# States' factors on VectorE instead of in TensorE's turns, and eight matmuls of zeros for each attention unit

## The chip, the cores and the metric

One core of a Trainium2 chip runs the whole kernel as one program. The metric is device time in microseconds; lower is better. The number for the kernel before is the median of three runs.

## The reference

Three stages follow one another. The attention reads x (4 batches, 8 heads, 512 tokens, 64 wide) against 32 states a head, both ways. The two results are joined to 2176 rows of 512. A dense layer with a Mish activation follows, and then a layer of eight experts of which each row takes the one with the best score.

```
scores = scale * x @ state.T ; a  = softmax(scores)  ; xread = a @ state
scores2 = scale * state @ x.T; a2 = softmax(scores2) ; sread = a2 @ x
x = concat([xread, sread]) as (2176, 512)
x = mish(x @ w_in) @ w_out
out = gate * (relu(x @ w1[e]) @ w2[e]),  e = argmax(cosine(x, expert_emb) / tau)
```

Both softmaxes divide by their sum plus 1e-9. The change touches only a2, the states' softmax.

## The kernel before

The attention is cut into eight units, one for each batch and half of the heads. A unit passes four steps. `s1` turns x on TensorE (tiles `xt`, copied to `xT` by ScalarE) and multiplies it by the turned states into the scores `sc`, which ScalarE copies to `ss`. `s2` makes both softmaxes: for the tokens' one GpSimd subtracts the maximum `mx`, ScalarE takes the exponential, GpSimd multiplies by the reciprocal sums `sm`. For the states' one TensorE turns the scores into `sb` (line 339), VectorE takes the maximum `mb` (line 342), ScalarE makes `a2` and the sums (line 346), and VectorE makes reciprocals of these (line 353). In the kernel before VectorE then makes a diagonal matrix `dg` of the reciprocals (line 355). `s3` turns `a` into `at` (line 368), and multiplies `a2` by `dg` into `a2t` (line 366), which turns and scales in one go. ScalarE copies that to `a2T` (line 371). `s4` multiplies it by x into `sr` (line 385), and VectorE places the result.

The loop over t calls `s1` of unit t, `s2` of unit t-1, `s3` of t-2 and `s4` of t-3, and one `convert_w`. It takes a block of the 64-bit weights w_in or w_out, loaded into one of two buffers, and makes two float parts of it: one pass on ScalarE (line 97), one on GpSimd (line 100), two on VectorE (line 71), and a split on ScalarE and GpSimd. Eight of 32 blocks are converted within the attention, the others beside the first steps of the dense layer.

The tiles that TensorE writes lie in few buffers. `xt`, `sb`, `at` and `a2t` of all units share four, under the tag `acc`; later the dense layer's sums lie there. `sc` has one buffer, shared with the first products of the dense layer (tag `ms`). A tile keeps its buffer from its first writer to its last reader.

The order of the instructions on each engine isn't that of the code. A planner lays them out ahead, up to the last part of the expert layer, by the durations that it assumes: an instruction goes to its engine's queue when its inputs and its buffer are due, the earliest in the code first. The order of each queue is fixed in the program. `warm(n)` is n matmuls of a 128x128 tile of zeros `wz` (bf16); it is called twice ahead of the units, with 30 each.

Of the kernel before, what the change touches and what calls it, by code (L numbers as in the profile page):

```python
# [8 lines left out]
F32 = mybir.dt.float32  # L9
# [6 lines left out]
ALU = mybir.AluOpType  # L16
# [5 lines left out]
P = 128  # L22
# [30 lines left out]
def body(tc, x, state, w_in, w_out, ee, tau, w1, w2, out):  # L53
    nc = tc.nc
    T, V, A, G, Y = nc.tensor, nc.vector, nc.scalar, nc.gpsimd, nc.sync
    stack = ExitStack()

    def pool(name, bufs=1, **kw):
        return tc.tile_pool(name=name, bufs=bufs, **kw)

    def tsc(o, i, s1, op0, s2=None, op1=None):
        if op1 is None:
            V.tensor_scalar(out=o, in0=i, scalar1=s1, scalar2=None, op0=op0)  # L63
        else:
            V.tensor_scalar(out=o, in0=i, scalar1=s1, scalar2=s2, op0=op0, op1=op1)
# [7 lines left out]
    def split(hi, lo, src, eng=None):  # L73
        A.activation(hi, src, AF.Copy)  # L74
        (eng or V).tensor_tensor(out=lo, in0=src, in1=hi.bitcast(F32), op=ALU.subtract)  # L75
# [34 lines left out]
    with stack:  # L110
# [7 lines left out]
        wz = const.tile([P, P], BF16, name="wz")  # L118
# [8 lines left out]
        ident = const.tile([P, P], F32, name="ident")  # L127
# [110 lines left out]
        def f32r(n, i, name):  # L238

            return xpool.tile([P, 512], F32R, tag=f"x{n}{i}", name=name)  # L240
# [25 lines left out]
        def attention(meanwhile):  # L266
            pa = ExitStack()
            tmp = pa.enter_context(pool("pa"))
# [21 lines left out]
            for h in range(4):  # L290
                q, r = divmod(h, 2)
                hs = slice(h * NST, (h + 1) * NST)
                o = SBD[hs, :, q, r * D : (r + 1) * D]
# [34 lines left out]
            def s2(u):  # L328
                d = ns[u]
                ss = d["ss"]  # L330
                v = ss.rearrange("p (g n) -> p g n", n=NST)
                mx = tmp.tile([P, 16], F32, tag="mx", bufs=2, name=f"mx{u}")
                V.tensor_reduce(mx, v, axis=AX, op=ALU.max)
                a = tmp.tile([P, 512], F32, tag="a", bufs=2, name=f"a{u}")
                av = a.rearrange("p (g n) -> p g n", n=NST)
                G.tensor_tensor(out=av, in0=v, in1=mx.unsqueeze(2).to_broadcast([P, 16, NST]), op=ALU.subtract)
                o = ps.tile([P, 512], F32, tag="acc", bufs=4, name=f"sb{u}")
                for j in range(KT):
                    T.transpose(o[:, j * P : (j + 1) * P], ss[:, j * P : (j + 1) * P], ident)
                A.activation(a, a, AF.Exp, scale=SCALE)  # L340
                mb = tmp.tile([P, 1], F32, tag="mb", bufs=2, name=f"mb{u}")
                V.tensor_reduce(mb, o, axis=AX, op=ALU.max)
                tsc(mb, mb, -SCALE, ALU.mult)
                a2 = tmp.tile([P, 512], F32, tag="a2", bufs=2, name=f"a2{u}")
                sb = tmp.tile([P, 1], F32, tag="sb", bufs=2, name=f"sbs{u}")
                A.activation(a2, o, AF.Exp, scale=SCALE, bias=mb, accum_out=sb)
                sm = tmp.tile([P, 16], F32, tag="sm", bufs=2, name=f"sm{u}")
                V.tensor_reduce(sm, av, axis=AX, op=ALU.add)
                tsc(sm, sm, 1e-9, ALU.add)
                V.reciprocal(sm, sm)  # L350
                G.tensor_tensor(out=av, in0=av, in1=sm.unsqueeze(2).to_broadcast([P, 16, NST]), op=ALU.mult)
                tsc(sb, sb, 1e-9, ALU.add)
                V.reciprocal(sb, sb)
                dg = tmp.tile([P, P], F32, tag="dg", bufs=2, name=f"dg{u}")
                tsc(dg, ident, sb, ALU.mult)
                d.update(a=a, a2=a2, dg=dg)

            def s3(u):
                d = ns[u]
                for n, key in enumerate(("a", "a2")):  # L360
                    o = ps.tile([P, 512], F32, tag="acc", bufs=4, name=f"{key}t{u}")
                    for j in range(KT):
                        js = slice(j * P, (j + 1) * P)
                        if n:

                            T.matmul(o[:, js], d[key][:, js], d["dg"], start=True, stop=True)
                        else:
                            T.transpose(o[:, js], d[key][:, js], ident)
                    if n:
                        t = d["a2T"] = tmp.tile([P, 512], F32, tag="a2T", bufs=2, name=f"a2T{u}")  # L370
                        A.activation(t, o, AF.Copy)
                    else:
                        if u < 2:
                            xh[0, u], xl[0, u] = f32r("h", u, f"xh0{u}"), f32r("l", u, f"xl0{u}")
                            split(xh[0, u], xl[0, u], o)
                        A.activation(AT[u // 2][:, u % 2, :], o, AF.Copy)
# [21 lines left out]
            for t in range(NU + 3):  # L398
                if t == 4:
                    load(3)  # L400
                if t < NU:
                    s1(t)
                if 0 <= t - 1 < NU:
                    s2(t - 1)
                if 0 <= t - 2 < NU:
                    s3(t - 2)
                if 0 <= t - 3 < NU:
                    s4(t - 3)
                for _ in range(t > 0):
                    if len(order) > len(order0) - FIRST:  # L410
                        convert_w()
                if t == 4:
                    embeddings(tmp)
                meanwhile(t)
# [579 lines left out]
        for g, (c, f) in enumerate(steps):  # L994
# [18 lines left out]
            if at == 2 and r:  # L1013
                pc, pf, _ = RUNS[r - 1]
# [130 lines left out]
```

## Time and profile before

| what | value |
|---|---|
| median of three runs | 733.88 us |
| the three runs | 731.34, 733.88, 737.31 us |
| the profiled execution | 731.85 us |
| its span in the trace | 730.1 us |
| granted TensorE clock, mean | 0.98 of full |

The span is the time from the first to the last instruction in the profile; 1.75 us of the profiled execution lie outside of it. PE is TensorE's matmul, PEld its weight load, DVE VectorE, ACT ScalarE, POOL GpSimd, SP the engine that issues loads. Times of the rows are microseconds from the start of the span, unless ns is given.

### The profile page before, as it was taken

How to read it: one execution, taken by the hardware profiler on the slowest of the kernel's cores; microseconds unless marked ns; L12 is line 12 of the kernel's file. 1: busy time of each engine (PE TensorE's matmuls, PEld its weight loads, DVE VectorE, ACT ScalarE, POOL GpSimd, SP SyncE). 2: the span in 40 equal slices, each digit the busy share in tenths (PEclk: the TensorE clock that was granted, in tenths of full speed). 3: DMA queues.
4: the chain of work that ended last, by engine and by line, in shares of the span. 5: the costliest groups of instructions: out<-in, count | busy, mean ns of one | idle time of the engine just before them, and what ended most of it. 6: DMA issues, size and time to landing. Idle time of an engine off the chain costs nothing.

```text
span 730.1 us, 11305 instructions
## 1 busy us (share of the span) xinstructions
PE 696.7 (95%) x3681; PEld 582.7 (80%) x3681; DVE 466.9 (64%) x969; ACT 456.3 (63%) x794; POOL 193.7 (27%) x165
## 2 busy tenths in 40 slices
PE   8789999999999999999999979799999999999994
PEld 8789877778888888888887867677888888888883
DVE  5987898897575865656567994573444752257741
ACT  5877989988697777656776776612434541246640
POOL 2785356651000210300002264212111312123101
PEclk9998999999999999999999999799999999999998
DMA  7652143430010100001000167305415631266530
GB/s 196 155 156 88 59 145 115 145 116 0 1 58 0 59 1 1 0 1 59 15 0 1 58 191 220 111 30 173 146 58 178 248 135 58 73 204 244 192 133 17
DMA packets 45499, 70.12 MB, mean 96 GB/s; under 512 B 23402, under 2 KB 23402, under 8 KB 45428
## 3 DMA queue, kind: packets, MB, share of 16 engines
q1 hardware_dynamic: 42068, 59.29, 25.2%
q0 software_dynamic: 3360, 9.99, 4.1%
q8 instruction: 31, 0.51, 0.3%
q14 instruction: 40, 0.33, 0.1%
HBM read 60.33 MB, written 9.98 MB: 96 GB/s over the span
## 4 chain that ended last, share of the span: by engine, by line
PE 40%; issue 24%; DMA 13%; DVE 9%; ACT 8%; POOL 3%; SPq 2%; POOLq 0%; DVEq 0%; ACTq 0%
DMA out<-ys,ix 8%; PE acc L106 6%; PE acc L107 6%; PE acc L108 6%; PE h L106 3%; PE h L107 3%; PE h L108 3%; DMA w<-in_moe_w_in 2%; DMA w<-in_moe_w_out 2%; DMA es<-in_moe_w 2%; PE lg L562 1%; SPq L285 1%; PE m L106 1%; PE m L108 1%; PE m L107 1%
## 5 line engine op out<-in xcount | busy, mean ns | idle before, releaser
L106 PE MATMUL acc<-woh,gh 128*128 128x512 f32 x272 | 110.0, 408 | 6.2 <-ACT gh L74 6.2
L107 PE MATMUL acc<-wol,gh 128*128 128x512 f32 x272 | 109.2, 403 | 0.0
L108 PE MATMUL acc<-woh,gl 128*128 128x512 f32 x272 | 95.9, 400 | 0.2 <-DVE gl L75 0.2
L936 POOL DMA_INDIRECT out<-ys,ix x21 | 21.1, 1007 | 195.4 <-DVE ys L63 187.9
L106 PE MATMUL hp<-w1h,xth 128*128 128x512 f32 x168 | 68.9, 410 | 0.0
L106 PE MATMUL y<-w2h,hth 128*128 128x512 f32 x168 | 68.0, 405 | 0.8 <-ACTq L877 0.8
L106 PEld LDWEIGHTS acc<-woh,gh 128*128 128x128 f32 x272 | 52.0, 191 | 20.1 <-ACT gh L74 9.1
L476 ACT ACTIVATE er<-h,mb__103 128x512 f32<-128x512 f32 x68 | 46.7, 686 | 33.8 <-PE h L108 31.7
L108 PE MATMUL hp<-w1h,xtl 128*128 128x512 f32 x168 | 67.3, 401 | 0.0
L107 PE MATMUL hp<-w1l,xth 128*128 128x512 f32 x168 | 67.2, 400 | 0.0
L107 PE MATMUL y<-w2l,hth 128*128 128x512 f32 x168 | 66.5, 396 | 0.4 <-DVEq L877 0.4
L108 PE MATMUL y<-w2h,htl 128*128 128x512 f32 x168 | 66.7, 397 | 0.0
L74 ACT ACTIVATE hth<-ht 128x512 fp32r<-128x512 f32 x42 | 23.0, 596 | 65.2 <-PE ht L920 62.0
L108 PEld LDWEIGHTS acc<-woh,gl 128*128 128x128 f32 x272 | 51.2, 190 | 13.0 <-DVE gl L75 1.8
L107 PEld LDWEIGHTS acc<-wol,gh 128*128 128x128 f32 x272 | 52.3, 192 | 11.0
L74 ACT ACTIVATE xth<-gt 128x512 fp32r<-128x512 f32 x21 | 12.4, 594 | 73.2 <-PE gt L894 73.2
L482 DVE TENSOR_TENSOR er<-er 128x512 f32<-128x512 f32 x56 | 40.0, 715 | 27.4 <-ACT er L476 27.4
L505 ACT ACTIVATE h<-er,mb__103 128x512 f32<-128x512 f32 x68 | 47.2, 695 | 10.5 <-DVE er L482 7.8
L106 PE MATMUL h<-xh,mh 128*128 128x512 f32 x128 | 51.2, 400 | 0.2 <-ACT xh L74 0.2
L107 PE MATMUL h<-xl,mh 128*128 128x512 f32 x128 | 50.4, 393 | 0.4 <-DVE xl L75 0.4
L108 PE MATMUL h<-xh,ml 128*128 128x512 f32 x128 | 50.2, 392 | 0.0
L506 ACT ACTIVATE er<-er,mb__103 128x512 f32<-128x512 f32 x68 | 49.2, 725 | 1.3
(435 smaller groups left out, 1704.7 us busy)
## 6 DMA issues: line engine op xcount, KB each, us to landing
sg<-in_moe_w SPq DMA_DIRECT2D x48, 512.0 KB, 6.4
w<-in_moe_w_in SPq DMA_DIRECT2D x16, 512.0 KB, 4.0
w<-in_moe_w_out SPq DMA_DIRECT2D x16, 512.0 KB, 3.3
es<-in_moe_w SPq DMA_DIRECT2D x32, 256.0 KB, 3.6
xn<-in_x SPq DMA_DIRECT2D x32, 128.0 KB, 3.4
x1d<-x SPq DMA_DIRECT2D x13, 256.0 KB, 3.4
x1d<-part SPq DMA_DIRECT2D x4, 256.0 KB, 2.9
xg<-x1d,perm POOLq DMA_INDIRECT x21, 3.7
```

The source lines that it names most:

```text
L74: A.activation(hi, src, AF.Copy)
L106: T.matmul(o, lh, rh, start=first, stop=False)
L107: T.matmul(o, lh, rl, start=False, stop=False)
L108: T.matmul(o, ll, rh, start=False, stop=last)
L285: Y.dma_start(XN[b][:, g, :, r * D : (r + 1) * D], src[g, r])
L476: A.activation(z, h, AF.Tanh, scale=0.5, bias=mb_[:, 0:1])
L482: V.tensor_tensor(out=z, in0=z, in1=z, op=ALU.mult)
L505: A.activation(r, z, AF.Square, scale=QS, bias=mb_[:, 1:2])
L506: A.activation(z, z, AF.Square, scale=QS, bias=mb_[:, 2:3])
L562: T.matmul(o[:, j], xt[:, k * P : (k + 1) * P], enT[:, k, :].unsqueeze(1).to_broadcast([P, 8, NE]), start=k == 0, stop=k == KT - 1)
L936: G.indirect_dma_start(out=out[:, :], out_offset=bass.IndirectOffsetOnAxis(ap=ix, axis=0), in_=y, in_offset=None, bounds_check=NTOK - 1, o ...
```

## The change

VectorE no longer makes the diagonal matrix. It multiplies `a2` (128x512) in place by the reciprocal sums, and TensorE turns `a2` in the same way as `a`. Ahead of the four turns of the scores of each unit, eight matmuls of zeros are written into the first quarter of the same tile `sb`, which the first turn then overwrites.

```diff
                 o = ps.tile([P, 512], F32, tag="acc", bufs=4, name=f"sb{u}")
+
+                for _ in range(8):
+                    T.matmul(o[:, 0:P], wz, wz, start=True, stop=True)
                 for j in range(KT):
                     T.transpose(o[:, j * P : (j + 1) * P], ss[:, j * P : (j + 1) * P], ident)
...
                 V.reciprocal(sb, sb)
-                dg = tmp.tile([P, P], F32, tag="dg", bufs=2, name=f"dg{u}")
-                tsc(dg, ident, sb, ALU.mult)
-                d.update(a=a, a2=a2, dg=dg)
+                tsc(a2, a2, sb, ALU.mult)
+                d.update(a=a, a2=a2)
...
-                        if n:
-
-                            T.matmul(o[:, js], d[key][:, js], d["dg"], start=True, stop=True)
-                        else:
-                            T.transpose(o[:, js], d[key][:, js], ident)
+                        T.transpose(o[:, js], d[key][:, js], ident)
```

## Rows read from the trace of the kernel before

**Rows 1.** Busy us by stage (instructions): PE, PEld, DVE, ACT, POOL; then granted clock.

```profile
17.50:62.00 44.50, 38.66 (x311) 37.05 (x310) 39.28 (x93) 34.43 (x70) 33.99 (x29) 0.92 0.55 156
62.00:165.00 103.00, 97.82 (x506) 80.11 (x505) 88.26 (x136) 93.52 (x168) 53.62 (x48) 0.98 0.32 108
165.00:420.00 255.00, 255.00 (x1318) 214.49 (x1318) 173.33 (x407) 185.26 (x327) 31.20 (x14) 1.00 0.06 18
```

**Rows 2.** Chain that ended last, from 17 to 67 us: start, length, what.

```profile
25.55 0.20 DVE dg L63
...
28.28 0.51 DVE dg L63
...
52.45 1.20 DVE dg L63
53.65 1.47 DVE wc07x L71
...
57.84 1.63 DVE wc10x L71
...
59.58 3.27 DMA w<-in_moe_w_out
```

**Rows 3.** Timeline of unit 2's turns: start us, length us, engine, instruction.

```profile
34.69 0.61 PE L368 MATMUL at<-ident,a 128*128 128x128 f32 x4
35.13 1.06 PE L366 MATMUL a2t<-dg,a 128*128 128x128 f32 x8
```

**Rows 4.** Line 63, VectorE, 15 to 70 us: ns min/median/max.

```profile
L63 DVE TENSOR_SCALAR sm<-sm x8: 156/174/1126, 15.0 to 67.3; 128x16 f32<-128x16 f32 x8
L63 DVE TENSOR_SCALAR sbs<-sbs x8: 140/153/154, 15.5 to 65.0; 128x1 f32<-128x1 f32 x8
L63 DVE TENSOR_SCALAR dg<-ident,sbs x8: 236/287/1200, 16.6 to 65.4; 128x128 f32<-128x128 f32 x8
L63 DVE TENSOR_SCALAR en<-en,er x1: 694/694/694, 36.1 to 36.1; 8x512 f32<-8x512 f32 x1
```

**Rows 5.** Groups by line and shape, 0 to 76 us: instructions, busy us, mean ns, idle.

```profile
L294 DVE COPY SBD<-stc 32x512 f32<-32x512 f32 x2 | 0.8, 420 | 0.1
```

**Rows 6.** Groups of VectorE alone, 17.5 to 62 us.

```profile
L63 DVE TENSOR_SCALAR dg<-ident,sbs 128x128 f32<-128x128 f32 x6 | 2.9, 476 | 0.0
```

**Rows 7.** Timeline of the start: the matmuls of zeros and the first turns.

```profile
0.99 4.43 PE L124 MATMUL wp<-wz 128*128 128x128 bf16 x52 [0.99 <-DVE wz L119]
...
5.25 0.60 PE L303 MATMUL st<-ident,SBD 128*128 128x128 f32 x4
...
7.12 0.50 PE L124 MATMUL wp<-wz 128*128 128x128 bf16 x6
```

**Rows 8.** Who waited for whom, 10 to 76 us: total us, times, longest.

```profile
PE xt L317 <- ACT a L346: 2.3, 1, 2.3
...
PE sb L339 <- ACT ss L325: 1.9, 1, 1.9
...
PE sb L339 <- ACT a2T L371: 1.4, 1, 1.4
```

**Rows 9.** Busy us around the low clock, columns as in Rows 1.

```profile
51.00:52.00 1.00, 0.00 (x0) 0.00 (x0) 1.00 (x3) 0.70 (x2) 0.43 (x1) 1.00 0.36 66
...
54.00:55.00 1.00, 1.00 (x11) 1.00 (x11) 1.00 (x1) 1.00 (x2) 0.92 (x2) 1.00 0.00 0
55.00:56.00 1.00, 1.00 (x7) 1.00 (x7) 1.00 (x3) 0.13 (x1) 0.83 (x2) 0.53 0.00 0
...
61.00:62.00 1.00, 1.00 (x7) 1.00 (x7) 0.96 (x4) 0.60 (x1) 0.00 (x0) 0.56 1.03 410
62.00:63.00 1.00, 1.00 (x11) 1.00 (x10) 1.00 (x3) 0.00 (x0) 0.00 (x0) 1.00 0.15 49
```

**Rows 10.** TensorE alone, 5.25 to 9 us: length, busy us (instructions), clock.

```profile
5.25:9.00 3.75, 3.75 (x41) 1.00 0.88 198
```

## The prediction

> **What bounds the kernel now.** I read the busy time by stage first, then the chain that ended last within the stage that the change touches, then the prices of its instructions, then who waits for whom there, then the clock. The stages differ. From 165 to 420 us TensorE is busy without a break [rows 1]; nothing that the change touches lies there, so that stage can only be moved as a block. From 62 to 165 us TensorE is busy for 97.8 of 103 us, ScalarE for 93.5 and VectorE for 88.3: 5.2 us of slack on TensorE. The attention's steady part is 17.5 to 62 us. VectorE is the fullest engine there, 39.3 of 44.5 us; TensorE shows 38.7, GpSimd 34.0 [rows 1]. In this part the chain that ended last passes mostly over VectorE, with loads of weights and GpSimd between: the diagonal matrix itself is on it at 25.55, 28.28 and 52.45 us, and the passes over the weights behind it [rows 2]. TensorE's turns aren't on it. So the stage goes at the pace of VectorE's queue, and this is where the change adds work; what it takes away is TensorE's.
>
> **The change part by part.**
>
> *Turns.* A unit's multiplication by the diagonal takes eight instructions and 1.06 us, the plain turn beside it four and 0.61 us [rows 3]. The change gives back 0.45 us of TensorE a unit, 8 x 0.45 = 3.6 us. As TensorE isn't on the chain, I count 0 of it.
>
> *Zeros.* Eight more matmuls of 128x128 a unit, 64 in all. At the start 52 of the same kind took 4.43 us, 85 ns each; six in a row took 0.50 us. One takes some 0.22 us from start to end, an estimate from 0.50 - 5 x 0.056, so six that follow each other by 56 ns fit too [rows 7]. A unit pays 8 x 0.056 = 0.45 to 8 x 0.085 = 0.68 us, all units 3.6 to 5.4 us. That eats what the plain turns save: TensorE's sum is 0 to +1.8 us, and its 5.8 us of idle time in the stage [rows 1] covers it. Without that cover it costs 1.8 us.
>
> *VectorE.* The diagonal (128x128) goes: median 0.287 us, mean 0.476 in the stage [rows 4, 6]. A product of 128x512 by a column comes. The nearest row is the same line with the same kinds of operands in place, 512 long: 0.694 us [rows 4]. Its length would leave no doubt, but it has 8 rows and is a single one beside a busy GpSimd. From below, a plain copy of 512 from the same memory took 0.420 us, at a time without GpSimd [rows 5]. From above, a pass of 512 long took 1.63 us in this stage [rows 2]. I take 0.694, as operation and operands are the same and GpSimd is busy for three quarters of the stage. A unit pays 0.694 - 0.287 = 0.41 us; from 0.420 it would be 0.13, and from 1.63 against the mean of 0.476 it would be 1.15. Six of the eight units have this step in the stage [rows 6]: 6 x 0.41 = 2.4 us, bounds 0.8 and 6.9. Three of these six stand on the chain now [rows 2], so 1.2 us is the least that I expect on the path; VectorE's 5.2 us of idle time can hide the rest. I take 1.8, the middle. The two other units lie outside of the stage and I count them at nothing: VectorE waits in the first, and in the last the dense layer's first steps run beside it; without that cover they add 0.8 us.
>
> A rule of the Trainium skill speaks for a lower price: VectorE: DVE Perf Modes, section Mode 2×_2P, says that a tensor-by-scalar operation between SBUF tiles runs at two elements a cycle even in fp32, since it reads one tensor through both ports. The copy of 0.420 us agrees and the product of 0.694 us doesn't, one instance each; by the rule the stage's 2.4 us would be 0.8.
>
> *Order within the unit.* The turn of `a2` now waits for the product instead of for the diagonal: 0.41 us later, and 0.45 us shorter. `a2T` is as late as before, and the product waits for nothing that the diagonal didn't wait for, so nothing new is queued behind it. No transfer is moved in the code.
>
> *Where the zeros land.* They need only `wz` and a free buffer under `acc`. The planner draws such instructions forward: of the 60 zeros of the two warm-ups, 52 run ahead of the first state turn, though 30 stand behind it in the code [rows 7]. So the eight zeros can stand well ahead of the turns of the scores, and `sb` then holds its buffer from there on. Buffers are short already: at 22.39 us the turns `xt` of a later unit waited 2.3 us for ScalarE's exponential over `sb`, its last reader, and once the turns of the scores waited 1.4 us for the copy of `a2t` [rows 8]. Both are waits for a buffer, as neither reads the other's data. Where the zeros meet such a wait, their 0.45 to 0.68 us comes behind it, ahead of the turns. I count one such case that VectorE doesn't hide, +0.5 us.
>
> *Sum.* 1.8 + 0.5 + 0 = +2.3 us at the end of the attention. TensorE's 5.2 us of slack from 62 to 165 us could swallow it, but ScalarE and VectorE are full there too [rows 1]; I let it through. The profiled execution of 731.85 us becomes 734.2; on the median, which lies 2.03 us higher, 733.88 + 2.3 = 736.2, and I forecast 736. The three runs of before span 6 us, so some 1% (7.3 us) is what can be told from no change.
>
> **The rivals.**
>
> *A: the zeros hold the buffers (slower).* Four buffers serve five tiles a unit. If `sb` takes one early in every unit, the wait of 2.3 us that is in the trace once comes back in others. For it: that row, and the pull forward of rows 7. Against it: `xt`, of the unit ahead, comes first in the code. It decides from three units on, since VectorE's slack of 5.2 us [rows 1] hides two. In five units it costs 5 x 2.3 = 11.5 us against the present layout: 745.
>
> *B: the zeros keep the clock up.* TensorE's clock falls to half from about 55 to 61.5 us and the instructions in a step of 1 us from 11 to 7; ahead of it TensorE did nothing from 51 to 52 us, where it waited 1.9 us for `ss` [rows 8, 9]. Eight zeros fill 0.45 to 0.68 us of that wait. If that holds the clock at 2.4 GHz, the 6.5 us at 1.2 GHz become 3.3, and up to 3.3 us are won if TensorE then leads. Against it: VectorE and a load are on the chain there [rows 2]. 736.2 - 3.3 = 732.9; with the cheap product (0.8 x 0.75 = 0.6 for 1.8) 731.7. I call it 732.
>
> *C: the turns let the clock fall.* From 5.25 to 9 us TensorE ran turns, zeros and the scores' matmuls at a granted clock of 1.00 [rows 10], and the one fall followed an idle stretch [rows 9]; the trace gives no sign that turns alone are too little. If they were, three more units would have a stretch like that from 55 to 61.5 us: 3 x 3.3 = 9.9 us of TensorE, of which its 5.8 us of idle time in the stage hides about half: 736.2 + 5 = 741. The Trainium skill, TensorE: Matmul & The Clock Gate, section Part 4: PE-mode transpose, has such a rule: turns aren't counted as activity as matmuls are, and the change makes turns of 32 products. By that rule the time is C's; rows 10 don't decide it, as real matmuls are among them.
>
> *D: a luckier layout.* The planner lays the whole program out anew, to the end of the dense layer. If the two buffer waits (2.3 + 1.4 us) and the wait for `ss` (1.9 us) fall away [rows 8], 5.6 us are won: 736.2 - 5.6 = 730.6, or 728 with the clock's 3.3 us where half of these overlap. More would have to come from 62 to 165 us, where TensorE has 5.2 us to lose.
>
> *E: nothing on the path.* VectorE's slack hides all of it: 734.
>
> **How the numbers follow.** Forecast 0.42 (733 to 739), E 0.12 (734), A 0.18 (740 to 746), C 0.07 (741), B 0.11 (732), D 0.10 (725 to 731). The range leaves out the outer parts of A and D: 727 to 746. Faster by over 1% is below 726.5: only the better third of D and layouts that I can't see, 0.08. Slower by over 1% is above 741.2: most of A, half of C, 0.18. Within 1%: 0.74.
>
> **What would show it.** The a2 product at line 63: near 0.69 us alone, or 0.42. The turns into `a2t`: four instructions, 0.61 us. In the stage to 62 us VectorE's busy time up by some 2 us and the dense layer's first `h` matmuls later by as much. For A: more waits of `xt` or `at` for ScalarE's exponential over `sb`, with the zeros far ahead of the turns in TensorE's queue. For B and C: the granted clock from 50 to 62 us, and at other places. The prediction is wrong if the new layout moves the loads of weights, and with them the end of the stage at 165 us, by more than the whole sum; or if TensorE, not VectorE, sets the pace of the units.

## The result and the profile after

The changed kernel takes 739.14 us (median of 12 runs, 734.51 to 742.68), the kernel before 732.37 us (12 runs beside them, 730.97 to 737.31): ratio 1.010, interval 1.0083 to 1.0116. It is slower by 6.8 us, clear of the noise. The forecast was +2.3 us, which the prediction itself put below what can be told from no change. The profiled execution of after took 739.43 us, span 737.7 us; the one of before 731.85 us, span 730.1 us.

**What came as worked out.** TensorE's part has the sizes of the forecast. The rows are from the timeline of after, unit 3 (columns as in [rows 3]; in brackets the idle time ahead and what ended it):

```profile
31.02 0.61 PE L340 MATMUL sb<-wz 128*128 128x128 bf16 x8 [1.51 <-ACT a2T L369]
31.47 0.61 PE L342 MATMUL sb<-ident,ss 128*128 128x128 f32 x4
...
35.88 0.60 PE L366 MATMUL a2t<-ident,a 128*128 128x128 f32 x4
36.31 0.60 PE L317 MATMUL xt<-ident,xn 128*128 128x128 f32 x4
39.49 1.09 PE L317 MATMUL xt<-ident,xn 128*128 128x128 f32 x4 [2.57 <-ACT a L349]
```

The turns into `a2t` are four instructions of 0.60 us where there were eight of 1.06 [rows 3]; eight zeros take 0.45 us to the next instruction. The 1.51 us that stood ahead of the turns of the scores [rows 8, 1.4 us] now stands ahead of the zeros, so these come behind the wait, not into it. One wait of `xt` for the exponential over `sb` is there, as before: it ends at 39.49 us instead of 22.39, and is 2.57 us long instead of 2.3.

VectorE's part came as worked out too, in its sum. The rows name the product `a<-a,sbs`, as the digits of names are left out (`a2` reads `a`). The first fence groups VectorE in the stage from 17.5 to 62 us (columns as in [rows 6]); the second is the busy time by stage (columns as in [rows 1]):

```profile
L63 DVE TENSOR_SCALAR a<-a,sbs 128x512 f32<-128x512 f32 x6 | 5.2, 870 | 0.0
```

```profile
17.50:62.00 44.50, 36.42 (x330) 34.67 (x328) 40.74 (x86) 32.28 (x66) 33.75 (x29) 0.96 0.54 145
62.00:165.00 103.00, 95.01 (x488) 77.59 (x488) 86.63 (x137) 90.52 (x163) 49.58 (x47) 0.98 0.32 108
165.00:420.00 255.00, 254.73 (x1307) 214.26 (x1308) 174.01 (x402) 186.16 (x329) 32.76 (x16) 0.99 0.05 16
```

Six products take 5.2 us where six diagonals took 2.9 [rows 6]: +2.3 us, forecast +2.4. The chain that ended last (start, length, what) shows what of it lies on the path, and what else does:

```profile
26.70 1.16 DVE a L63
...
29.22 1.04 DVE a L63
...
33.76 4.26 DMA w<-in_moe_w_in
38.10 0.35 ACT wc04x L97
38.66 0.78 ACT a L349 x2
39.49 1.09 PE xt L317 x4
...
41.09 0.96 PE sb L340 x8
...
45.12 1.80 PE sc L323 x16
...
55.05 1.40 DVE a L63
...
59.23 3.14 DMA w<-in_moe_w_out
```

The products on the chain are 3.60 us, the diagonals were 1.91 [rows 2]: +1.7 us, forecast 1.8. Between them stands what the forecast had at 0.5 us: a load of weights that lands at 38.02 us, the conversion `wc04x` that waited for it on ScalarE, the exponential queued behind that, and the turns `xt` that wait for the exponential.

What the forecast had not: from 39.49 to 46.92 us the chain stays on TensorE, with the eight zeros of a unit on it for 0.96 us, and TensorE's granted clock is at half from 39.6 to 43.0 us. In a second trace of the same kernel (e8, below) the chain is on TensorE from 39.37 to 55.94 us, with the clock at half from 39.0 to 52.7. In the two traces of the kernel before TensorE has nothing, and 2.5 us, of the chain from 17 to 60 us.

**Where the time is.** I cut each trace at two instructions of TensorE: the start of the first matmul of the routing scores `lg`, and the start of the last product `m` on line 106. Behind that `m` come the last sums of the dense layer and the experts' part, to the end of the span. From `lg` to `m` it is 197.4 to 197.6 us in every kernel of this study: that block only moves. The rows of after for `lg` and `m` (each with its first and last start), and those of before:

```profile
L560 PE MATMUL lg<-enT,xt x8: 217/274/275, 220.8 to 225.7; 128*128 128x64 f32 x8
L106 PE MATMUL m<-wih,STh x128: 277/281/562, 64.4 to 418.3; 128*128 128x256 f32 x128
```

```profile
L562 PE MATMUL lg<-enT,xt x8: 217/274/276, 215.9 to 220.8; 128*128 128x64 f32 x8
L106 PE MATMUL m<-wih,STh x128: 277/281/448, 61.7 to 413.4; 128*128 128x256 f32 x128
```

So 4.9 us are lost by there, and 737.7 - 418.3 = 319.4 against 730.1 - 413.4 = 316.7 us from `m` on: 2.7 us more are lost in a part that the change doesn't touch. Two further profiled executions (e7 and e8, below), of before (217.5, 316.8) and of after (220.4, 319.4), give means: an early loss of 3.9 and a late one of 2.65 us, 6.6 of the 6.8 measured. The late values of a kernel agree within 0.2 us, the early ones of before differ by 1.6.

The two pairs of traces don't lose the early part in the same way. Up to `lg`, TensorE is idle for 13.6 us in before's first trace and 17.6 in after's, and the low clock takes 5.1 us in both (one less the granted clock, summed). In the second pair it is idle for 15.5 us in both, and the low clock takes 3.4 us in before and 6.8 in after. So no one wait is shown to be the early loss. The first sum `acc` of the dense layer starts at 81.0 and 84.2 us in before and at 84.1 and 86.4 in after: on the mean 2.65 of the 3.9 us are there already. From it to the last `m`, TensorE's order is the same in both kernels.

The late loss can be read from the timeline. First before, then after, TensorE and GpSimd around the second hand-over to the experts:

```profile
494.10 0.60 PE L654 MATMUL po<-ph,Q 128*128 128x44 bf16 x17
...
499.75 0.60 PE L894 MATMUL gt<-ident,xg 128*128 128x128 f32 x4
496.13 0.98 POOL L889 DMA_INDIRECT xg<-x1d,perm  x1 [6.26 <-issue]
```

```profile
500.57 0.60 PE L652 MATMUL po<-ph,Q 128*128 128x44 bf16 x17
...
504.12 0.40 PE L108 MATMUL y<-w2h,htl 128*128 128x512 f32 x1
506.07 0.63 PE L892 MATMUL gt<-ident,xg 128*128 128x128 f32 x4 [1.55 <-DMA xg<-x1d,perm]
502.60 0.98 POOL L887 DMA_INDIRECT xg<-x1d,perm  x1 [8.32 <-issue]
```

In both the gather `xg` is issued 2.03 us behind the start of the `po` matmuls. But after starts `po` 82.3 us behind the start of the last `m`, before 80.7, and has fewer matmuls left to run under the gather: 13 products stand between `po` and `gt`, where before has 21, and TensorE is idle for 1.55 us. The instructions are the same; the planner set them in another order. This wait is some 1.55 us of the late 2.65. From `m` to `gt` it is 86.3 and 86.6 us in before's two traces, 87.8 and 89.1 in after's; from `gt` to the end 230.3 and 230.3, and 231.6 and 230.35. In after's first trace the clock fell behind the wait, in the second it didn't. The rest of the late loss isn't placed.

### The profile page after: what moved, and what is told of

It is laid out like the page before. It is cut to its first block, busy times and chain, and to the rows that moved or that the text cites. A ratio compares the mean times of both kernels' runs of the same rounds, so it can differ in the third digit from the quotient of the medians.

```text
span 737.7 us, 11367 instructions
## 1 busy us (share of the span) xinstructions
PE 697.9 (95%) x3713; PEld 582.5 (79%) x3713; DVE 470.7 (64%) x969; ACT 457.3 (62%) x794; POOL 192.3 (26%) x165
## 4 chain that ended last, share of the span: by engine, by line
PE 39%; issue 25%; DMA 14%; ACT 9%; DVE 8%; POOL 2%; SPq 2%; POOLq 0%; DVEq 0%; ACTq 0%
DMA out<-ys,ix 7%; PE acc L106 6%; PE acc L107 6%; PE acc L108 6%; PE h L106 3%; PE h L107 3%; PE h L108 3%; DMA es<-in_moe_w 3%; DMA w<-in_moe_w_in 2%; PE lg L560 1%; PE m L106 1%; SPq L285 1%; PE m L108 1%; PE m L107 1%; DMA w<-in_moe_w_out 1%
```

## The experiments

The theories: Z, the early loss comes with the zeros; V, it comes with VectorE's product; L, both losses belong to the layout that the planner makes of the whole program, whatever was changed to bring it on. Times are medians; each ratio is to the kernel before on the same chip. In the table, early is the start of the first `lg` less 216.7 us (the mean of before's two), late is `m` to the end less 316.75 us, each from one profiled execution. That execution can lie off its kernel's median (e6 by +3.2 us, e3 +2.4, e1 and e10 +2.2, e12 -1.8), so early and late together needn't give the loss of the runs, and differences of some 2 us between kernels in these columns show little.

| kernel | us | ratio, interval | early | late |
|---|---|---|---|---|
| after (two profiled) | 739.1 | 1.010, 1.0083 to 1.0116 | +4.1, +3.7 | +2.7, +2.7 |
| e1 zeros, diagonal kept | 741.3 | 1.0109, 1.0081 to 1.0137 | +8.6 | +2.2 |
| e2 product, no zeros | 739.4 | 1.0093, 1.0057 to 1.0129 | +0.8 | +7.2 |
| e3 turns twice, no zeros | 732.6 | 0.9995, 0.9976 to 1.0015 | +1.2 | +1.1 |
| e4 16 zeros | 740.9 | 1.012, 1.0098 to 1.0142 | +6.5 | +2.2 |
| e5 before, 24 for 30 | 735.0 | 1.003, 1.0009 to 1.0051 | +0.5 | +1.8 |
| e6 after, 44 for 30 | 740.9 | 1.0109, 1.0075 to 1.0142 | +8.7 | +2.7 |
| e9 product, no zeros, 20 for 30 | 736.6 | 1.0059, 1.0032 to 1.0087 | +1.9 | +2.9 |
| e10 4 zeros | 737.9 | 1.0067, 1.0041 to 1.0092 | +3.2 | +4.3 |
| e11 zeros, own buffer | 736.1 | 1.0037, 1.0015 to 1.006 | +3.8 | -0.6 |
| e12 after, 22 for 30 | 736.0 | 1.004, 1.0021 to 1.006 | -0.8 | +2.3 |

**One part alone.** e1 is the kernel before with the eight zeros; e2 is the changed kernel without them.

```diff
 e1, against before
+                for _ in range(8):
+                    T.matmul(o[:, 0:P], wz, wz, start=True, stop=True)
```

> The kernel before with the eight matmuls of zeros a unit, and the diagonal kept. Theory V (VectorE sets the pace, so the product is the cost): 732 to 734, as VectorE gets nothing new. Theory Z (the zeros' time and the buffer that they hold are the cost): 737 to 741, all of the 6.8 us. Theory L (a new layout of what follows the attention costs about half of it, whatever change causes it): 734 to 737, with a late shift beside the early one.

> The changed kernel without the zeros: in-place product and plain turns alone. Theory V: 737 to 740, nearly all of the loss, and the first matmul of the dense layer some 2 us later than in the kernel before. Theory Z: 731 to 734, TensorE has less work. Theory L: 734 to 737.

Each alone costs about as much as both together (L's 734 to 737 was missed by both), so the parts don't add up, as prices of their own would. And they lose in different places: the zeros early, the product late. With the product and without zeros the first `m` starts at 61.8 us, as in before (61.7): V, by which the product paces the units, gives at most 0.8 us here, though the time of 739.4 us is what V had foretold. In e1 part of the loss stands where no zeros are; the waits of its TensorE from 10 to 226 us, and those of before to 216 us:

```profile
PE acc L106 <- ACT gh L74: 9.6, 5, 5.1
PE at L370 <- POOL a L353: 4.0, 4, 1.9
```

```profile
PE acc L106 <- ACT gh L74: 4.4, 5, 1.8
```

The dense layer's sums wait 5.2 us more, in a stage behind the attention whose order of instructions was set anew in e1.

**The zeros' time and their number.** e3 takes the zeros out and turns the scores twice instead: four more turns, the same 0.45 us of TensorE, but they need `ss` and so can't be drawn forward. e4 doubles the zeros.

```diff
 e3, against after
-                for _ in range(8):
-                    T.matmul(o[:, 0:P], wz, wz, start=True, stop=True)
-                for j in range(KT):
+                for j in 2 * list(range(KT)):
```

> The changed kernel with the four turns of the scores made twice in place of the eight zeros: the same 0.45 us of TensorE a unit, but they need the scores, so they can't stand early nor hold the buffer early. Theory V: 738 to 741, as the changed kernel. Theory Z, by the buffer: 732 to 735; by the time alone: 738 to 741. Theory L: anywhere from 732 to 741, by its late layout.

> The changed kernel with sixteen zeros a unit instead of eight: 3.6 us more of TensorE. Theory V: 738 to 741, the zeros are hidden. Theory Z: 742 to 748, as much again. Theory L: no order between this and the changed kernel.

e3 has the product, the plain turns and TensorE's extra 0.45 us a unit, and its time is that of before. (Its profiled execution, from which the table's +1.2 and +1.1 are, lies 2 us above the mean of its runs.) So the product and that much of TensorE's time need not cost anything; that this layout won back what they cost isn't excluded. e4, twice the zeros, is 1.8 us above after, with intervals that overlap, and its early loss (+6.5) is less than that of e1 (+8.6) with half as many; as much again for twice the zeros, Z's 742 to 748, is not borne out.

**Only the layout.** The second warm-up's count of zeros is changed (it stands behind the start, and most of these matmuls run at the start). e5 is the kernel before with 24 for 30, by which TensorE's order behind the last `m` becomes that of after; e6 is the changed kernel with 44 for 30, by which it becomes that of before.

```diff
-            warm(30)
+            warm(24)
```

> The kernel before, with its diagonal and without zeros among the units; only the second warm-up has 24 matmuls of zeros instead of 30. The planner then lays out the instructions behind the dense layer's last products on TensorE exactly as it does for the changed kernel, and those from the first sums of the dense layer to its last products as in both kernels. Theory L (the late layout costs 2.5 to 3 us): 735 to 736, with a wait for a gather just above 500 us and the clock at half behind it, and plan's matmuls ahead of it later. Theory N (the change's own instructions are the cost): 732 to 733, six zeros less are nothing.

> The changed kernel, with 44 matmuls of zeros in the second warm-up instead of 30. The planner then lays out the part behind the dense layer's last products on TensorE as in the kernel before. Theory L: 736 to 737, some 3 us less than the changed kernel, and no wait for the gather above 500 us; by up to 1 us more, as 14 zeros stand ahead of the first state turns. Theory N: 739 to 740.

e5 is slower by 2.1 us, as L had it, and nothing of the change is in it: it shows the wait of `gt` for the gather (1.5 us) and a late loss of 1.8. e6 missed what was expected by either theory: its wait of `gt` for the gather is gone, yet its late part is no shorter: from 425 to 530 us the low clock takes 8.5 us of it (one less the granted clock, summed over rows of 1 us), where it took 6.8 in before and after. And its attention got an order of its own that starts `lg` at 225.4 us, 4 to 5 us later than after.

To see how much of this is chance of one execution, both kernels were profiled again:

> The kernel before once more, for a second trace. From the first state turn to the dense layer's first product 56 us as in the first trace, and from there to the first routing scores 154 us, each within 1 us, if the stages are as steady as the whole (some 0.3%). If the stages wander by 2 us from run to run, no single trace can place the loss.

> The changed kernel once more, for a second trace. If the loss has its places in the program: 58 us from the first state turn to the first product, 156 us from there to the first routing scores, and again the wait for a gather just above 500 us with the clock at half behind it. If the places are chance: other stages carry the loss.

Before gave `lg` at 217.5 us and 731.8 us of span, after 220.4 and 737.3. In after's second trace the first products stand at the same places and the wait of `xt` is 2.7 us, and the wait for the gather is there again (1.6 us). But the places within the early part did not repeat to 1 us. Before's second trace took 155.7 us from the first `m` to `lg` where its first took 154.2, and after's took 61.2 and 153.5 us for the two stages where its first took 58.4 and 156.4. Nor did the clock fall behind the gather. As pairs of traces the early loss is 4.9 and 2.9 us, the late one 2.7 and 2.6.

**Zeros, their buffer, and the same zeros in another order.** The last four. e9 has no zeros, e10 has four, e12 eight; in all three TensorE's order from the dense layer's first sums to the end is that of after. e11 writes after's zeros to a buffer under `h`, so that they hold none under `acc`.

```diff
 e11, against after
+                oz = ps.tile([P, P], F32, tag="h", bufs=3, name=f"zz{u}")
+                for _ in range(8):
+                    T.matmul(oz, wz, wz, start=True, stop=True)
                 o = ps.tile([P, 512], F32, tag="acc", bufs=4, name=f"sb{u}")
-                for _ in range(8):
-                    T.matmul(o[:, 0:P], wz, wz, start=True, stop=True)
```

> The product on VectorE and the plain turns, no zeros ahead of the turns of the scores, and the second warm-up cut from 30 to 20 matmuls, by which TensorE's order from the dense layer's first sums to the end is that of the changed kernel. Theory Z (the early loss of the change, some 4 us to the first routing scores, comes with the zeros; the late one, 2 to 3 us, with the order behind the last products): early loss 0 to 1 us, the time that of the kernel before with the same late order, 735 (734 to 737). Theory V (VectorE's product paces the attention): early loss 2 to 4 us, 737 to 740. Theory L (no part has a price of its own; every layout has its own time): anything from 732 to 741, and the early loss is not tied to the zeros.

> The changed kernel with four zeros in place of eight; TensorE's order from the dense layer's first sums to the end is that of the changed kernel. Theory Z by their time: half the early loss, some 2 us, 737 (735.5 to 738.5). Theory Z by the buffer that they take early (one zero takes it as well as eight): early loss 4 us, 739. Theory V: 739, early loss 4 us, since the product is the same. Theory L: anything from 733 to 741.

> The changed kernel with its eight zeros written to a tile of their own in the three buffers under h, so that they hold none of the four under acc; the planner gives it an order of its own in all parts. If the loss comes from holding a buffer of acc early: early loss 0 to 1 us, no zeros that wait for the reader of another tile in acc, 733 to 737 by its late part. If it comes from the zeros' time on TensorE: early loss 4 us, 738 to 741. Theory L: anything from 733 to 742.

> The changed kernel with the second warm-up cut from 30 to 22 matmuls: the same eight zeros and the same product, TensorE's order from the dense layer's first sums to the end is that of the changed kernel, its order within the attention is another. Theory Z: early loss 3 to 5 us, late loss 2 to 3 us, 739 (737 to 741). Theory L: the early loss goes with the order within the attention, so it may be anything from 0 to 9 us, 733 to 744.

By its time e9 fits Z (734 to 737), though its early 1.9 us is more than the 0 to 1 that Z gave it. e9 to e10 to after, the early loss grows with the zeros, 1.9, 3.2, 3.9, and taken alone would have borne out Z. e12 ends that: the same zeros, the same product, the same order behind the attention, and no early loss in its trace. By 12 runs it is 3.1 us faster than after, below Z's range, and the intervals of the two ratios are apart. (Its trace is of a run 1.8 us below its median; by the runs, 3.5 us of loss less the late 2.3 leave some 1.2 early.) With e5 this gives what order alone is worth, some matmuls of the warm-up aside: 3.1 us from e12's order in the attention to after's, 2.1 us from before's order to e5's, 5.2 of the 6.8. And e12, with the whole change, and e5, with none of it, lie 1.1 us apart with intervals that overlap. e12's TensorE waits from 10 to 216 us:

```profile
PE acc L106 <- ACT gh L74: 3.3, 5, 1.4
PE sb L340 <- ACT a2T L369: 2.2, 2, 1.4
PE at L366 <- POOL a L354: 1.8, 2, 1.1
PE xt L317 <- ACT a L349: 1.2, 1, 1.2
PE sb L342 <- ACT ss L325: 1.1, 1, 1.1
```

against, in after to 221 us:

```profile
PE acc L106 <- ACT gh L74: 5.9, 5, 1.8
PE sb L342 <- ACT ss L325: 3.2, 2, 2.7
PE xt L317 <- ACT a L349: 2.6, 1, 2.6
PE sb L340 <- ACT a2T L369: 1.5, 1, 1.5
PE at L366 <- POOL a L354: 1.4, 1, 1.4
```

What after waits longer for than e12 is ScalarE (`xt`, `sb` for `ss`, `acc` for `gh`). Two of these can be followed: in after the exponential at 38.66 us and the copy into the last `ss` at 63.02 us stand on ScalarE behind conversions of weights that waited for their loads; in e12 the last copy stands at 61.56 us, ahead of its conversion. This is one trace each: in after's second, `acc` waits 4.4 us, as in before, and `ss` is waited for 1.8 us, while before's second has 4.7 us of that. Only the longer wait of `xt` is in both, and before has one of 2.3 and 2.1 us. So the waits that e12 is spared aren't shown to be the early loss. e12's six products are cheap as well:

```profile
L63 DVE TENSOR_SCALAR a<-a,sbs 128x512 f32<-128x512 f32 x6 | 3.0, 492 | 0.1
```

e11 speaks against the buffer as the price: with zeros that hold nothing under `acc` the early loss of its trace is after's (+3.8), in another wait (3.7 us, the first `m` for the copy into `ss`). Its time of 736.1 us alone would have fitted the buffer theory (733 to 737). Its late part is the shortest of all; there `po` starts 80.2 us behind the start of the last `m` and `gt` doesn't wait:

```profile
498.30 0.60 PE L652 MATMUL po<-ph,Q 128*128 128x44 bf16 x17
...
503.96 0.60 PE L892 MATMUL gt<-ident,xg 128*128 128x128 f32 x4
500.33 0.98 POOL L887 DMA_INDIRECT xg<-x1d,perm  x1 [6.26 <-issue]
```

The seven profiled executions with after's late order (both of after, e2, e5, e9, e10, e12) all show this wait, 1.5 to 1.6 us, and their `po` ends 82.9 to 85.7 us behind the start of the last `m`; none of those of before, e3 and e11 does, and they have 80.8 to 81.5. e1, e4 and e6, with other late orders (e6 with before's), wait at most 0.2 us there, but their `po` ends at 83.6 to 84.0: on the way to it the low clock takes 8.5 us, before 6.8. So a late `po` can come from the clock as well. No kernel of the study beats the kernel before; e3 takes the same time.

## Why the prediction was wrong

- *Turns, zeros on TensorE, net 0:* right in size, 0.60 us and 0.45 us a unit, and e3 spends the same TensorE time and takes the time of before. The premise, TensorE isn't on the chain, held for before and not for after: there TensorE has 7.4 and 16.6 us of it in the attention, with zeros among them. The prediction named this as a sign of being wrong (TensorE sets the pace). It comes with the low clock and isn't the zeros' doing alone: in e5, without any, the chain is on TensorE from 38.6 to 52.7 us, at half clock.
- *VectorE's product, 2.4 us in the stage and 1.8 on the path:* the numbers came out for the layout that was timed, 2.3 and 1.7, but by luck. As a price of the product they are wrong: the nearest row (0.694 us) held a wait, and the products of after are long by waits for GpSimd as well (below). Alone the product takes 0.40 to 0.48 us, the diagonal 0.23 to 0.30: some 0.2 us more each, 1.2 for six. e12, where it is mostly alone, pays 3.0 us for the six, 0.1 more than the diagonals of before [rows 6], some of which waited. The Trainium skill, VectorE: DVE Perf Modes, section Mode 2×_2P, which the forecast set aside for that row, had the better price for it; by it the stage's term was 0.8.
- *Zeros that meet a buffer wait, +0.5:* mis-sized. In after the moved wait of `xt` (2.57 us) is on the chain, where the one of before was not. It ends with a load of weights and ScalarE's queue, though, not with a buffer that zeros hold. The early loss less the product's term is 3.9 - 1.7 = 2.2 us where 0.5 stood; this is a remainder, and no wait was found that makes it up. Rival A in its form (several waits of 2.3 us for the buffers) didn't happen, and e11 takes its mechanism away without taking the early loss away.
- *The sum passes through to the end:* this is the step that failed. It took everything behind the attention as moved, not changed, without a reason, and a new layout only as luck (rival D), and only to the end of the dense layer, though the planner goes on to the last part of the expert layer. The sum of 2.3 became 3.9 early, and the 0 behind it became 2.65 us late. A wait of 1.55 us at a hand-over 430 us behind the last attention unit is the part of it that can be followed, and e5 shows 1.8 us of late loss in the kernel before with nothing of the change in it. The prediction's sign of being wrong ("the new layout moves the loads of weights") looked no further than 165 us; a worse layout had no chance and no price of its own. The ten kernels tried ran from the time of before to 8.8 us above it, so the kernel before is at the good end of the layouts seen here; whether most others would lose too, these few don't show.
- *Rival B:* not borne out, falls of the clock are still there after the change, and before's second trace has none from 55 to 61.5 us either (its fall is at 62.6). *Rival C:* not borne out either; e3 has more plain turns than after and the least time at the low clock in its runs (mean granted clock 0.985, before 0.982, after 0.978). The rule that goes with C, from the Trainium skill, TensorE: Matmul & The Clock Gate, section Part 4: PE-mode transpose, isn't decided by that: no run here is turns alone.

What stays open: which step of the planner turns eight zeros into the order of after's attention. Why the early loss of the kernels with zeros lies mostly between 3 and 9 us and that of those without between 0.5 and 2 isn't settled by one counter-example, e12; with it, the zeros are no sufficient cause, but they may make a bad order likelier. Which waits make up after's early loss, and where 1.1 of the late 2.65 us go, stays open too.

## What to carry to other kernels

Where a planner orders the whole program, a small edit is two changes: its own price, here too small to be told from nothing, and a new layout, with which the kernels of this study took up to 9 us of 732 more; before one part is blamed, time the kernel before under a change that does nothing but re-order (e5). A part's loss that vanishes with the part isn't yet shown to be its price: e9, e10 and after gave a clean rise with the zeros, and e12 with all of them gave 3.1 us back. Look at hand-overs far behind the edit for work that no longer covers a transfer.

## What the runs showed of the hardware

**A product that meets GpSimd mostly ends just behind it.** How long the product takes goes by what GpSimd does when it starts. Rows of after's timeline, VectorE and GpSimd at two places:

```profile
46.03 0.40 DVE L63 TENSOR_SCALAR a<-a,sbs 128x512 f32<-128x512 f32 x1
55.05 1.40 DVE L63 TENSOR_SCALAR a<-a,sbs 128x512 f32<-128x512 f32 x1
```

```profile
46.25 1.07 POOL L354 TENSOR_TENSOR a<-a,sm 128x512 f32<-128x512 f32 x1 [1.62 <-DVE sm L353]
...
54.90 1.27 POOL L75 TENSOR_TENSOR wil<-wc06x,wih 128x512 fp32r<-128x512 f32 x1
```

At 46.03 us GpSimd's instruction starts later, and the product takes 0.40 us. At 55.05 one is running, till 56.17, and the product ends at 56.45: 0.28 us behind it. Of after's eight products five end 0.28 to 0.29 us behind an instruction of GpSimd that ran when they started (those of 0.66, 1.24, 1.04, 1.40 and 0.85 us); the diagonal of before did the same, 0.08 us behind (1.20 us at 52.45 [rows 2]). So most of the length of such a product is GpSimd's, and a longer product adds about 0.2 us whether it meets one (0.28 against 0.08 us behind it) or not (0.47 against 0.27 us alone; an estimate from the product at 25.56 us in e12 and the diagonal at 36.54 us in e5). The Trainium skill, SBUF — State Buffer, section SBUF: two separate sides, has the rule: the port pair that the two engines share goes to whichever starts first, a GpSimd instruction or a VectorE instruction that uses both ports, for its whole length, and the other is blocked. The traces agree, with these 0.28 us, but not by the starts that they record: in e4 and e6 products that started 0.01 to 0.04 us ahead of GpSimd's instruction waited for it too (0.95 to 1.37 us), and in e12 one that started 0.17 us behind GpSimd's, at 38.41 us, took 0.47 us and ended 0.91 us ahead of it; there GpSimd's had started while another instruction of VectorE ran.

**The clock fell behind a wait, but not behind the same wait each time.** TensorE's granted clock around after's wait at 36.9 to 39.49 us (columns as in [rows 9]):

```profile
38.00:39.00 1.00, 0.00 (x0) 0.00 (x0) 0.48 (x3) 0.90 (x2) 0.75 (x2) 1.00 1.21 227
39.00:40.00 1.00, 0.51 (x3) 0.52 (x4) 1.00 (x3) 1.00 (x4) 1.00 (x1) 0.78 1.11 215
...
42.00:43.00 1.00, 1.00 (x7) 1.00 (x6) 0.54 (x3) 0.39 (x1) 1.00 (x2) 0.52 0.80 193
43.00:44.00 1.00, 1.00 (x12) 1.00 (x11) 0.80 (x2) 0.57 (x2) 1.00 (x2) 1.00 0.96 360
```

It falls to 1.2 GHz as work comes back, for 3.4 us here. Behind the wait of `gt` for the gather it fell in three of the seven traces (e2 and e10 for 7 us, the first of after for 3.5 us) and not in four, so what the same wait costs wanders. From `gt` to the end before takes 230.3 us; the four of the seven without a fall take 230.35 to 230.9, the three with one 231.6 (3.4 us at low clock) and 233.0 to 233.1 (6.8 us).

Over all runs the low clock takes (1 - 0.9782) x 737.6 = 16.1 us in after. In before it takes (1 - 0.9818) x 731.0 = 13.3 us, by the 28 runs beside e9 to e12. This is no price: TensorE isn't on the chain all the time. Among runs of one kernel, one with 1 us more of it was 0.55 us longer (an estimate, by a line through the 163 runs, each less the mean of its kernel on its chip), so the 2.8 us between the two kernels stand for some 1.5 of the 6.6 us between their spans. e12 has 16.1 us as well, so its gain on after isn't the clock's. For others the clock is a large part: in e2, e9 and e10 it takes 5.4 to 7.4 us more than in before on the same chip, some 3 to 4 us by this estimate, of losses of 4.0 to 7.0 us; in e5 1.9 us more, some 1.0 of its 2.1.
